# One DMA transpose per batch of the attention output, in place of one for each half of the heads

## The chip, the cores and the metric

One core of a Trainium2 chip runs the whole program. The metric is the device time of one execution in microseconds (us). The kernel before takes 726.11 us, the median of three runs (722.44, 726.11 and 727.01 us). The profiled execution took 723.2 us, and its span, from the first to the last instruction that the profile shows, is 721.4 us.

## The reference

Attention over 8 batches, 8 heads, 576 positions and 64 channels, with two kinds of mask, and after it a mixture of 8 experts in which each token goes to one expert and each expert takes 576 tokens:

```
mask_local = (rel >= 0) & (rel < 32)                        # heads 0 to 3
mask_strided = (rel >= 0) & (pos_k % 32 == pos_q % 32)      # heads 4 to 7
attn_out = softmax(mask(q k^T / 8)) v
x = attn_out.transpose(0, 2, 1, 3).reshape(4608, 512)       # one row per token
logits = x @ w_gate                                         # 4608 by 8
# pairs (token, expert) in falling order of logit; a pair is taken if the token
# is free and the expert has fewer than 576 tokens
out[mask_e] = relu(x[mask_e] @ w1[e]) @ w2[e]
```

Columns 0 to 255 of x come from the local heads and columns 256 to 511 from the strided heads.

## The kernel before, in words

**Units and steps.** The attention is cut into 16 units (`Unit`, L265): unit 2b is the four strided heads of batch b and unit 2b+1 its four local heads. Each unit is worked in two steps, one for each pair of heads. The loop at L609 runs over the steps i from -1 to 31, and everything in it is a schedule written out by hand: in step i TensorE does the scores of pair i+1 (`dots`, L353), the products with v of pair i (`mix`, L397), and the start of the scores of pair i+2. VectorE takes maxima (L357, L366), builds the shift (L371) and norms the result (L412 to L415); ScalarE takes the exponentials (L380). Work that belongs to no step of its own is put into lists by step (`at`, `drips`, `mids`, L530 to L565).

**What each unit moves.** `load` (L305) brings k, q and v for a unit three units ahead, at the start of an even step, on SP's queue (L312, L313, L319, L323). k and q of a kind have two buffers, and so has v, so a load must wait until the unit two of its kind before has been used. `finish` (L421) cuts the unit's result into a 16-bit high part and a low part (ScalarE L427, GpSimd L428). `store` (L430) writes both into the scratch tensor `x_scr` in HBM, whose row for a token holds 2 by 512 values: the second index of its shape is the column half, 0 for local and 1 for strided, and each half has 256 high and 256 low values. A strided unit's store is six transfers (L440), three from SP and three from GpSimd (four and two for the last strided unit); a local unit's is two from SP (L444, L445).

**The transposes.** `turn` (L447) reads a unit's half of the batch's rows back from `x_scr` as 576 by 512 and writes it transposed into an SBUF tile `xts` or `xtl` of 128 partitions by 4 by 576. One runs for each unit but the last: eight strided and seven local. `gates` (L459) multiplies both tiles of a batch with the gate's weights on TensorE (L465) and `logits` (L509) sums them up. The last batch's local half is transposed on TensorE (L481) instead, and its logits are made by `last_part` (L492).

**The order on SP's queue.** SP takes its instructions strictly in program order and stops at the first that has to wait. From the lists, the order for batches 0 to 4 is, over and over: transpose of strided unit 2b; store of local unit 2b+1; load of strided unit 2b+4; transpose of local unit 2b+1; store of strided unit 2b+2; load of local unit 2b+5. The lists put a unit's transpose four steps after the unit's first step for units 0 to 9, three for units 10 to 13 and one for unit 14 (L565). A batch's `gates` runs in step 4b+9 up to batch 4, in step 28 for batch 5 and in step 30 for batch 6.

**After the attention** comes a search for the expert's tokens (L768), then the experts one after another: the tokens are gathered (L1072), transposed 128 rows by 1024 at a time (L1075 by DMA, L1060 on TensorE), and multiplied (L1159, L1207), with the weights loaded and cut at L987 to L1021. The change doesn't touch this part.

Of the kernel before, what the change touches and what calls it, by code (L numbers as in the profile page):

```python
# [9 lines left out]
F16 = mybir.dt.float16  # L10
# [8 lines left out]
B, H, S, D = 8, 8, 576, 64  # L19
# [113 lines left out]
def band_stride_attention_then_capacity_moe(ctx, tc, qt, kl, ks, nl, ns, wg, w1, w2, cst, out, dbg=None):  # L133
    nc = tc.nc
# [8 lines left out]
    x_scr = dram.tile([N, 2, DM], F16, name="x_scr")  # L143
# [76 lines left out]
    with tc.tile_pool(name="ld", bufs=2) as ld, \  # L220
# [44 lines left out]
        class Unit:  # L265
# [71 lines left out]
            def room(u, p):  # L337
                u.sp[p] = ps_a.tile([128, 2, BANK], F32, name="spa")
# [106 lines left out]
                    nc.sync.dma_start(xs[n:, 0], xo[:S - n, n // 128])  # L445

            def turn(u):  # L447
                j = 1 if u.strided else 0
                u.xt = wk.tile([128, 2, 2, S], F16, name="xt" + u.g)
                nc.sync.dma_start_transpose(u.xt.rearrange("p a d n -> p (a d) n"), x_scr[u.b * S:(u.b + 1) * S, j])  # L450

        HB = S // 2
        ltb, gs = {}, {}
# [1 line left out]
        def gate_scale(b):  # L455
            gs[b] = wk.tile([128, 1], F32, name="st")
            nc.vector.tensor_scalar(gs[b], vscale[b][0][:, 1:2], sg[:, 1:2], None, op0=OP.mult)

        def gates(b, po):  # L459
            lt = ltb[b] = wk.tile([128, S], F32, name="lt")  # L460
            xts = (todo[2 * b + 1].xt, todo[2 * b].xt)
            for a in range(2):
                for j in range(2):
                    for k in range(4):
                        nc.tensor.matmul(po[32 * k:32 * k + 32, j, :HB], wgh[:, k].rearrange("p a e -> p (a e)"),  # L465
                                         xts[k // 2][:, a, k % 2, j * HB:(j + 1) * HB],
                                         start=(a == 0), stop=(a == 1), skip_group_check=True)
            nc.scalar.activation(lt.rearrange("e (j n) -> e j n", j=2), po[:, :, :HB], AF.Copy, scale=gs[b])
# [40 lines left out]
        def logits(b, po):  # L509
            po = po[:, :5 * E].rearrange("q (c e) -> q c e", e=E)  # L510
            sp = spans(b)
            for k, (r, _, tok) in enumerate(sp):
                nc.tensor.matmul(po[r, k], ltb[b][:, tok], sum_g, start=(k == 0), stop=(k == 4), skip_group_check=True)
            c = sp[0][1]
            nc.vector.tensor_copy(L[:, c:c + 4], po[:, :4])
            r, c, _ = sp[4]
            nc.vector.tensor_copy(L[r, c], po[r, 4])
# [8 lines left out]
        todo = [Unit(b, strided) for b in range(B) for strided in (True, False)]  # L526
        nu = len(todo)
        fills = {}

        def at(step, f, early=False):  # L530
            q = fills.setdefault(max(step, 0), [])
            q.insert(0, f) if early else q.append(f)
# [6 lines left out]
        for j, u in enumerate(todo):  # L539
            if j == 1:  # L540
                for k in range(6):
                    drips.setdefault(k // 3, []).append(lambda u=u, k=k: u.copy_v(k))
                for p in range(2):
                    drips.setdefault(2, []).append(lambda p=p: todo[0].rescale(p))
            if j > 1:
                if not u.strided:
                    for k in range(6):
                        drips.setdefault(2 * j + COPY_AT[k], []).append(lambda u=u, k=k: u.copy_v(k))
                    for f in range(2):
                        at(2 * j - V_AT + f, lambda u=u, f=f: u.square_v(f), True)  # L550
                else:
                    at(2 * j - V_AT_S, u.square_v, j > 2)
                if not u.strided:
                    mids2[2 * j - 3] = u
                    drips.setdefault(2 * j - 2, []).append(u.scale_v)
            if not u.strided and u.b < B - 1:
                at(2 * j + (4 if u.b < B - 2 else 3), lambda k=u.b: gate_scale(k))
                if u.b < B - 2:
                    mids.setdefault(2 * j + (7 if u.b < B_LATE else G5), []).append(lambda a, b, k=u.b: gates(k, a))
                (mids if u.b == B - 2 else mids3).setdefault(2 * j + (L_AT if u.b < B_LATE else G5 + 1 if u.b < B - 2 else 5), []).append(lambda a, b, k=u.b: logits(k, b))  # L560
            for p in range(2):
                at(2 * j + p if j else 2, lambda u=u, p=p: u.finish(p, nc.gpsimd))
            at(2 * j + (2 if j < nu - 2 else 1), u.store)
            if u is not todo[-1]:
                at(2 * j + (4 if j < 2 * B_LATE else 3 if j < nu - 2 else 1), u.turn)  # L565
        todo[0].load(v=False)
        for u in todo[:2]:
# [12 lines left out]
        def pair(i):  # L580
            return (todo[i // 2], i % 2) if 0 <= i <= last else None
# [27 lines left out]
        for i in range(-1, 2 * nu):  # L609
            u, n, m = pair(i), pair(i + 1), pair(i + 2)  # L610
# [7 lines left out]
            if m or i in mids:  # L618
                a = room(m) if m else ps_a.tile([128, 2, 512], F32, name="spa")
# [446 lines left out]
    def tokens(ph, idx):  # L1066
        xt = xp.tile([128, 2 * 2 * 2, CAP], F16, name="xt")
        for t in range(NT):
            n = min(128, CAP - 128 * t)
            xg = xp.tile([128, 2 * DM], F16, name="xg", bufs=5)  # L1070
            with urgent(ph):
                nc.gpsimd.indirect_dma_start(out=xg[:n], out_offset=None, in_=x_rows,  # L1072
                                             in_offset=bass.IndirectOffsetOnAxis(ap=idx[:n, t:t + 1], axis=0))
                if ph or t >= TURNS:
                    nc.sync.dma_start_transpose(xt[:, :, t * 128:t * 128 + n], xg[:n])  # L1075
                else:
                    first.append(lambda t=t, n=n, xg=xg: turn(xt, xg, t, n))
        return xt.rearrange("p (a j d) n -> p a j d n", a=2, j=2)
# [252 lines left out]
```

## Time and profile before

| | |
|---|---|
| median of 3 runs | 726.11 us |
| the profiled execution | 723.2 us |
| its span | 721.4 us |
| TensorE (PE) busy over the span | 625.3 us, 87% |
| VectorE, ScalarE, GpSimd busy | 455.9, 320.8, 153.7 us |
| mean granted clock of TensorE | 0.893 |
| the attention, by the last transposes of `last_part` (L496) | up to 220 us |
| transposes by `turn` (L450) | 8 + 7 on SP's queue |

How to read it. PE is TensorE's matmuls, PEld its weight loads, DVE VectorE, ACT ScalarE, POOL GpSimd and SP SyncE; a name with a q behind it (SPq, POOLq) is that engine's queue of DMA issues. L397 is line 397 of the kernel. In a row of waits the columns are the time waited in all, the number of times and the longest one. In a row of the timeline they are the start, the duration, the engine, the line, the operation, what is written and read, and in brackets the idle time in front of it and what ended it. In a row of the table by windows they are the window and its length, then the busy time of each engine with its number of instructions, the granted clock, the mean busy share of the 16 DMA engines and GB/s. Rows of DMA queues give packets, megabytes and the share of 16 engines' time that the packets took; it can pass 100% where packets overlap.

### The profile page before, as it was taken

The numbers are of one execution on the slowest core, as the hardware profiler recorded it, in microseconds if no ns is written. First come the engines' busy times: TensorE is split into PE (matmuls) and PEld (weight loads), VectorE is DVE, ScalarE is ACT, GpSimd is POOL, SyncE is SP. The second block draws the span as 40 slices with busy tenths as digits, with TensorE's granted clock in tenths as the row PEclk, the third lists the DMA queues.
The fourth block names the chain that finished last, engine by engine and source line by source line (L and its number), as shares of the span: only waits on it lengthen the run. The fifth ranks groups of instructions, "written<-read, shape, count | busy, mean of one in ns | idle before, by whom it ended". The sixth has DMA issues, their size and how long they took to land.

```text
span 721.4 us, 19211 instructions
## 1 busy us (share of the span) xinstructions
PE 625.3 (87%) x8040; PEld 402.7 (56%) x8043; DVE 455.9 (63%) x1368; ACT 320.8 (44%) x497; POOL 153.7 (21%) x152
## 2 busy tenths in 40 slices
PE   6986978889993479999989998989989998699993
PEld 3664756566663346557537646646644744555741
DVE  4786666786876777867657767757666573662200
ACT  3634634653520156473454364274184265753210
POOL 2053323332330020140040040041041023202011
PEclk9667787985885589999999999999999999899998
DMA  9999999999651360680680491392196079551010
GB/s 248 263 256 221 248 262 260 232 247 214 113 134 50 122 200 1 218 213 2 223 194 15 146 254 33 105 265 63 35 295 103 1 271 262 182 96 52 1 38 29
DMA packets 111401, 111.21 MB, mean 154 GB/s; under 512 B 76332, under 2 KB 84102, under 8 KB 110803
## 3 DMA queue, kind: packets, MB, share of 16 engines
q1 hardware_dynamic: 103235, 88.44, 47.7%
q0 software_dynamic: 7360, 21.15, 9.9%
q8 instruction: 63, 1.03, 0.6%
q10 hardware_dynamic: 720, 0.39, 0.2%
q14 instruction: 23, 0.19, 0.1%
HBM read 73.59 MB, written 18.87 MB: 128 GB/s over the span
## 4 chain that ended last, share of the span: by engine, by line
PE 29%; issue 16%; DVE 7%; DMA 6%; ACT 3%; SPq 3%; POOL 2%; another core or an unknown queue 1%; POOLq 0%; ACTq 0%
PE ph L1159 16%; PE ph L1207 9%; DMA w<-in_w_dram 4%; SPq L1075 2%; DVE w2l L1021 2%; ACT jk L1002 2%; DMA xg<-x_scr,idx 2%; POOL out_dram L1218 1%; DVE w1l L1021 1%; DVE hl L1167 1%; PE ph L1201 1%; POOL xg L1072 1%; SPq L987 1%; PE ph L1060 0%
## 5 line engine op out<-in xcount | busy, mean ns | idle before, releaser
L1159 PE MATMUL ph<-xt,w1h 128*128 128x288 f16 (+2 forms) x1024 | 180.0, 288 | 7.0 <-DMA xt<-xg 4.4
L1218 POOL DMA_INDIRECT out_dram<-y,idx x40 | 43.5, 1087 | 351.3 <-ACT y L1217 324.8
L1159 PEld LDWEIGHTS <-w1h 128*128 128x128 f16 x1024 | 97.1, 98 | 34.5 <-issue 6.7
L1159 PE MATMUL ph<-xt,w1l 128*128 128x288 f16 (+2 forms) x512 | 113.3, 288 | 0.0
L1002 ACT ACTIVATE jk<-w 128x1024 f16<-128x1024 f32 x64 | 67.5, 1055 | 73.2 <-DMA w<-in_w_dram 69.3
L1207 PE MATMUL ph<-w2l,hh 128*128 128x512 f16 x256 | 97.9, 382 | 0.0
L1207 PE MATMUL ph<-w2h,hh 128*128 128x512 f16 x256 | 97.7, 382 | 0.0
L1207 PE MATMUL ph<-w2h,hl 128*128 128x512 f16 x256 | 97.7, 382 | 0.0
L1166 ACT ACTIVATE hh<-ph 128x576 f16<-128x576 f32 (+2 forms) x72 | 42.8, 595 | 120.2 <-PE ph L1159 119.2
L1207 PEld LDWEIGHTS <-hh 128*128 128x128 f16 x512 | 48.7, 98 | 58.0 <-issue 9.5
L1167 DVE SCALAR_TENSOR_TENSOR hl<-ph,hh 128x576 f16<-128x576 f32 (+2 forms) x72 | 49.5, 688 | 43.7 <-ACT hh L1166 43.4
L380 ACT ACTIVATE pr<-spa 128x576 f32<-128x576 f32 x32 | 20.8, 650 | 93.9 <-PE spa L376 89.4
L1159 PEld LDWEIGHTS <-w1l 128*128 128x128 f16 x512 | 49.9, 98 | 12.6 <-issue 0.6
L397 PE MATMUL po<-v_s,pr 64*54 64x65 f32 (+1 forms) x768 | 45.6, 276 | 10.2 <-issue 6.5
L428 POOL TENSOR_TENSOR xos<-xs,xos 118x768 f16<-118x768 f32 x16 | 27.2, 1701 | 119.8 <-ACT xos L427 87.8
L1217 ACT ACTIVATE y<-ph,so 128x512 f32<-128x512 f32 x32 | 21.9, 684 | 67.7 <-PE ph L1207 48.1
L1072 POOL DMA_INDIRECT xg<-x_scr,idx x40 | 40.5, 1012 | 50.2 <-issue 34.7
L1021 DVE SCALAR_TENSOR_TENSOR w1l<-w,w_sw,w1h 128x512 f16<-128x512 f32 x64 | 45.7, 745 | 8.0 <-issue 4.6
L1021 DVE SCALAR_TENSOR_TENSOR w2l<-w,w_sw,w2h 128x512 f16<-128x512 f32 x64 | 45.7, 742 | 7.9 <-ACT y L1217 6.8
L397 PEld LDWEIGHTS po<-v_s,pr 64*54 64x54 f32 (+1 forms) x768 | 34.7, 162 | 17.2 <-issue 11.7
L1207 PEld LDWEIGHTS <-hl 128*128 128x128 f16 x256 | 25.1, 98 | 33.2 <-issue 8.1
L1020 ACT ACTIVATE w1h<-w,w_sw 128x512 f16<-128x512 f32 x64 | 41.8, 710 | 3.9 <-DVE ss_e L203 1.8
(613 smaller groups left out, 961.9 us busy)
## 6 DMA issues: line engine op xcount, KB each, us to landing
w<-in_w_dram SPq DMA_DIRECT2D x64, 512.0 KB
kl<-in_kl_dram SPq DMA_DIRECT2D x16, 304.0 KB
v_s<-in_ns_dram SPq DMA_DIRECT2D x16, 292.5 KB
v_l<-in_nl_dram SPq DMA_DIRECT2D x16, 292.5 KB
ks<-in_ks_dram SPq DMA_DIRECT2D x16, 288.0 KB
qs<-in_qt_dram SPq DMA_DIRECT2D x16, 288.0 KB
ql<-in_qt_dram SPq DMA_DIRECT2D x16, 288.0 KB
x_scr<-xol SPq DMA_DIRECT2D x8, 512.0 KB
```

The lines of the kernel that those rows point to most:

```text
L397: nc.tensor.matmul(po[r:r + n, j - j0], pr[k, o:o + n], u.vn[k, t, 2 * p + h], start=(j == j0), stop=(j == j1 - 1), skip_group_check=True)
L428: eng.tensor_tensor(u.xo[:nr, :, 1, c], xf, u.xo[:nr, :, 0, c], op=OP.subtract)
L1002: nc.scalar.activation(jk, wf[:, c * n4:(c + 1) * n4].rearrange("p c f -> p (c f)"), AF.Square, scale=1.41422, accum_out=sq[:, c:c + 1])
L1020: nc.scalar.activation(hi[:, c, f], wf[:, c, f], AF.Copy, scale=s_)
L1021: nc.vector.scalar_tensor_tensor(lo[:, c, f], wf[:, c, f], s_, hi[:, c, f], op0=OP.mult, op1=OP.subtract)
L1072: nc.gpsimd.indirect_dma_start(out=xg[:n], out_offset=None, in_=x_rows, in_offset=bass.IndirectOffsetOnAxis(ap=idx[:n, t:t + 1], axis=0))
L1159: nc.tensor.matmul(tile_[:, j, :w], wt[:, d, f * 128:(f + 1) * 128], xt[:, d // 2, xx, d % 2, c], start=(k == 0), stop=(k == 3 * DC - 1))
L1166: nc.scalar.activation(hv, src, AF.Relu)
L1167: nc.vector.scalar_tensor_tensor(lv, src, 0.0, hv, op0=OP.max, op1=OP.subtract)
L1207: nc.tensor.matmul(py, a[:, f, ts_], w[:, f], start=(k == 0), stop=(k == len(todo) - 1))
L1217: nc.scalar.activation(y, py, AF.Copy, scale=so[:, t:t + 1])
L1218: st = nc.gpsimd.indirect_dma_start(out=out_rows, out_offset=bass.IndirectOffsetOnAxis(ap=idx[:n, t:t + 1], axis=0), in_=y[:n], in_offset= ...
```

## The change

The transpose of a strided unit is dropped. When the local unit of the batch is due, one transpose reads both halves, 576 rows by 1024 values, and writes both into one tile `xt` of 128 partitions by 2 by 4 by 576, of which there are two buffers; `gates` reads its two halves as before. The two tiles of 4,608 bytes for each partition and two buffers each become one tile of 9,216 bytes with two buffers, so the room in SBUF is the same. The last strided unit, whose local half is never transposed by DMA, keeps its own transpose of 576 by 512.

```diff
             def turn(u):
-                j = 1 if u.strided else 0
-                u.xt = wk.tile([128, 2, 2, S], F16, name="xt" + u.g)
-                nc.sync.dma_start_transpose(u.xt.rearrange("p a d n -> p (a d) n"), x_scr[u.b * S:(u.b + 1) * S, j])
+                j = slice(1, 2) if u.strided else slice(0, 2)
+                xt = wk.tile([128, 2, 2, 2, S], F16, name="xt", bufs=2)
+                nc.sync.dma_start_transpose(xt[:, j].rearrange("p j a d n -> p (j a d) n"),
+                                            x_scr[u.b * S:(u.b + 1) * S, j].rearrange("n j f -> n (j f)"))
+                u.xt = xt[:, 1]
+                if not u.strided:
+                    todo[2 * u.b].xt, u.xt = xt[:, 1], xt[:, 0]
...
-            if u is not todo[-1]:
+            if not u.strided and u.b < B - 1 or j == nu - 2:
                 at(2 * j + (4 if j < 2 * B_LATE else 3 if j < nu - 2 else 1), u.turn)
```

On SP's queue the order becomes: store of local unit 2b+1; load of strided unit 2b+4; transpose of batch b; store of strided unit 2b+2; load of local unit 2b+5. Fifteen transposes become seven of double width and one of the old width.

## The prediction

> **What bounds the kernel now.** I read the page first, then the table by windows, the waits of TensorE, the timelines of TensorE and SP, and at last the DMA queues in short windows.
>
> ```profile
> PE 625.3 (87%) x8040; PEld 402.7 (56%) x8043; DVE 455.9 (63%) x1368; ACT 320.8 (44%) x497; POOL 153.7 (21%) x152
> DMA  9999999999651360680680491392196079551010
> q8 instruction: 63, 1.03, 0.6%
> ```
>
> The DMA engines are full in the first ten of 40 slices, up to 180 us. Queue 8 carries 63 packets, 1.03 MB: one packet of 16 KB for every 255 of TensorE's 16,083 instructions. I read it as TensorE's instruction fetch. Now a stretch around the transpose of local unit 1:
>
> ```profile
> 60.00:66.00 6.00, 5.49 (x175) 3.95 (x165) 5.65 (x17) 4.06 (x5) 3.79 (x4) 1.00 1.16 228
> 66.00:72.00 6.00, 0.23 (x7) 0.17 (x6) 1.82 (x7) 0.00 (x0) 0.72 (x1) 0.78 1.14 226
> 72.00:78.00 6.00, 6.00 (x121) 4.28 (x122) 3.02 (x6) 2.85 (x4) 0.15 (x1) 0.50 1.07 240
> ```
>
> TensorE sets the pace of the attention: where it runs it is busy for 5.5 to 6.0 of 6 us, longer than any of the others but VectorE in the first row. From 66 to 72 us it stands still, the others run out of work behind it, and afterwards its granted clock is half. The waits of TensorE between 40 and 170 us:
>
> ```profile
> PE po L397 <- issue: 10.2, 8, 5.8
> ```
>
> It waits for nothing that the profile names, in the middle of a group of like matmuls:
>
> ```profile
> 65.51 0.54 PE L397 MATMUL po<-v_s,pr 64*54 64x65 f32 x11
> 71.83 1.03 PE L397 MATMUL po<-v_s,pr 64*54 64x65 f32 x13 [5.77 <-issue]
> ...
> 94.23 0.25 PE L353 MATMUL spa<-qs,ks 64*18 64x18 f32 x4 [2.91 <-issue]
> ...
> 117.90 0.44 PE L353 MATMUL spa<-qs,ks 64*54 64x54 f32 x8 [1.56 <-DMA x_scr<-xos]
> ```
>
> The queues in four short windows, 61 to 69, 69 to 70.5, 86.2 to 91.5 and 91.5 to 93 us, in this order:
>
> ```profile
> q0 software_dynamic: 167, 0.28, 21.6%
> ...
> q8 instruction: 1, 0.02, 4.7%
> ...
> q1 hardware_dynamic: 2473, 1.45, 117.3%
> ...
> q0 software_dynamic: 182, 0.28, 53.1%
> ...
> q8 instruction: 1, 0.02, 4.2%
> ```
>
> In these windows a local transpose moves, by its 2,304 packets of 256 B from 62.5 to 69.5 and from 88.3 to 91.9 us. The first and the third window have no row of queue 8, so no fetch is served there; one comes as each transpose ends, takes 1.1 us (4.7% of 16 engines in 1.5 us), and TensorE goes on 2.3 us behind the end of the transpose (69.5 to 71.83, 91.9 to 94.23). In the third window GpSimd's stores, issued at 87.28 us, have no row either, and 182 packets right after it. So a transpose holds the DMA engines to its end, and TensorE runs out of instructions behind it. I take the wait before 117.90 us, behind the local transpose of batch 2, for the same, though the profile puts it down to a store. No stall of this list stands behind a strided transpose: there the fetch is late too, but TensorE still had instructions left.
>
> The Trainium skill (Runtime: NRT & Kernel Launch, Instruction fetch mechanics) says that instructions come in blocks of 16 KiB, 256 to a block, and that crossing into the next is mostly hidden. The trace agrees on the block; on the hiding it differs, by 5.77 us. If the page held here, the length of a transpose would cost nothing and the sum below would be 0.
>
> **The change part by part.** SP's queue around batches 0 and 1, then GpSimd's stores:
>
> ```profile
> 48.60 3.42 SPq L450 DMA_TRANSPOSE xts<-x_scr  x1
> 53.35 2.20 SPq L323 DMA_DIRECT2D v_s<-in_ns_dram  x4
> 58.77 5.51 SPq L450 DMA_TRANSPOSE xtl<-x_scr  x1
> ...
> 80.25 1.91 SPq L323 DMA_DIRECT2D v_s<-in_ns_dram  x4
> 84.44 5.90 SPq L450 DMA_TRANSPOSE xtl<-x_scr  x1
> ...
> 59.26 2.08 POOL L440 DMA_DIRECT2D x_scr<-xos  x3 [0.30 <-POOL xos L428]
> 87.28 1.99 POOL L440 DMA_DIRECT2D x_scr<-xos  x3 [0.30 <-POOL xos L428]
> ```
>
> *Data.* 576 by 512 values are 589,824 B, 2,304 packets of 256 B. 8 x 2,304 + 7 x 2,304 packets before, 7 x 4,608 + 2,304 after: the same 34,560, since a row is cut into 256 B either way. Its cost is not the bytes but how long one piece lasts.
>
> *Length of one piece.* An undisturbed one, 203.5 to 206.4 us, and the flow in 110.5 to 115.3 us:
>
> ```profile
> 203.50:206.40 2.90, 2.48 (x81) 2.15 (x84) 2.72 (x11) 1.34 (x2) 0.00 (x0) 0.91 1.00 203
> ...
> GB/s 384 365 346 384 422 365 442 384 384 365 442 384 365 442 365 365 326 405 341 303 233 230 190 164 68 30 36 28 203 292 288 292 288 292 288 292 288 292 288 292
> ```
>
> The flow dips, some 1.5 us, while engines finish their loads one by one, then runs at 290 GB/s. Another 589,824 B take 2.0 us at 290 GB/s. A double transpose lasts 4.9 us alone (2.9 + 2.0) and 5.6 under load (3.6 + 2.0). SP's issue grows from 2.29 us (the shortest) to between 2.29 and 4.58; I take 4.2, since a part is fixed.
>
> *What moves.* The strided transpose no longer stands ahead of the local store and the strided load. It waits for TensorE's last product of the unit two of its kind before, here units 2 and 4:
>
> ```profile
> 49.36 1.67 PE L397 MATMUL po<-v_s,pr 64*54 64x65 f32 x24
> ...
> 78.95 1.27 PE L397 MATMUL po<-v_s,pr 64*54 64x65 f32 x24
> ```
>
> Unit 4's ends at 80.2 us and the load goes out at 80.25: it is held by TensorE, not by SP. So in batches 1 to 4 it comes no earlier, though its data meet an emptier queue, which I put at 0.5 us. Unit 2's ends at 51.0 us and the load went out at 53.35: in batch 0 it can go 2.3 us earlier, and with the 0.5 us the transpose can start to move at 59.8 us in place of 62.5.
>
> *Stalls, batch by batch*, each from both sides:
>
> - Batch 0: now 5.8 us. This transpose took 7.0 us against 3.6 because GpSimd's stores (issued at 59.26) were under way and got between: 167 packets of queue 0 above. Started at 59.8 us it is ahead of them, as batch 1's was, starting 1.0 us behind the issue. Then it ends at 59.8 + 5.6 = 65.4 us, and TensorE, dry at 66.05, goes on at 67.7: 1.6 us, a gain of 4.2. If the stores get between after all: 2.0 us longer. Ends: -4.2 and +2.0; I take -4.2.
> - Batches 1 and 2: the end moves by 2.0 - 0.5 and the stall with it, one for one: +1.5 each, between 0 and +5 (2.0, and 3.4 for stores in between).
> - Batches 3 and 4: no stall stands behind their transposes now, so part of the 2.0 us is covered by what TensorE has left. Ends 0 and +2.0 each; I take +0.5 and +1.0.
> - Batches 5 and 6: the DMA engines are at half load there. 0 to +1 together; +0.5, half way.
>
> Sum: -4.2 + 1.5 + 1.5 + 0.5 + 1.0 + 0.5 = +0.8 us.
>
> *At nothing.* The strided half is later, but only `gates` reads it:
>
> ```profile
> 202.18 2.63 SPq L450 DMA_TRANSPOSE xtl<-x_scr  x1
> ...
> 209.43 0.42 PE L465 MATMUL spa<-xtl,wgh 128*32 128x288 f16 x2
> ```
>
> The schedule leaves three steps between a batch's transpose and its `gates` up to batch 4, and one for batch 6, the tightest: issued at 202.18, moving from 203.5, landed by 208.4 (203.5 + 4.9), used at 209.43; without that cover it costs up to 1 us, inside batch 6's bound. The store of unit 2b+2 and the local load behind the transpose go out up to 4.6 us later; but loads run three units ahead and the transpose of the strided unit that used to stand in front of the next ones is gone, so they are covered; if they were not, the delay would be those 4.6 us. SP's waits for strided stores ahead of a transpose vanish; nothing behind them was late.
>
> The profiled execution took 723.2 us, so the sum gives 724.0 us for it. That execution lies 2.9 below the median of 726.1, so I forecast 726.9 us for the median.
>
> **The rivals.**
>
> *Longer stalls (slower).* Batch 0 gains nothing because GpSimd's stores still get in, and each loaded double transpose puts its full 2.0 us on TensorE: 5 x 2.0 = 10.0 us. Two more stalls (batches 3 and 4) each bring a stretch at half clock: 121 matmuls in 6 us against 175, a loss of 1.9 us, together 3.7. Sum +13.7, about 740 us. For it: the stalls end with the transpose wherever it is seen. Against it: batches 3 and 4 had room left. It decides from the point where the stall in batch 0 is not below 5.8 us. In a mild form (+8) it gives 734.
>
> *Fetches slip in between (faster).* If the double transpose is served in pieces, the extra half adds no blocking: batches 1 to 6 add 0, batch 0 gains 4.2, and the half clock behind it (if 10 us at a loss of 1.9 in 6) goes too, 3.2. Sum -7.4, 718.7 us. For it: the flow dips at the start of each transpose, where others get in. Against: no queue-0 or queue-8 packet in the last 3 us of the one at 88.3 us.
>
> The Trainium skill (DMA: Bandwidth & Descriptors, Queues, rings and completion order) says that an engine goes round its queues packet by packet, at most 64 descriptors each, and so speaks for this rival. By it a fetch would wait for 64 descriptors at most, not for a whole transpose; no run here shows such a change of queue within the steady flow.
>
> *Nothing that can be told (no effect).* TensorE's stalls move about and come out even, or the one instruction is worked as two halves: 723 to 730 us. This holds my own sum too.
>
> **How the numbers follow.** The three runs differ by 4.6 us, so about 1%, 7.3 us, is what can be told from no change. My sum and its neighbours: 0.60. Longer stalls: 0.25, from the two batches in which the end of the transpose and of the stall are seen together. Fetches slip in: 0.15. Faster by over 1% is the second rival's 0.15, slower the first's 0.25. The range must reach into both: from 717 (the faster rival and 1.6 us of scatter) to 739 (the slower one, all but its last us).
>
> **What would show it.** Right: seven transposes of some 5 to 6 us of movement in the short windows, no queue-8 packet inside them and one right behind; the idle time in L397 near 66 us at 1 to 2 us in place of 5.77; those near 94 and 118 us longer by about 1.5 us; 34,560 packets as before; the last product of `gates` no later by more than 1 us against its neighbours. Wrong: stalls of 4 us or more behind most double transposes (the first rival), or queue-8 packets within them and stalls below 3 us (the second). If the stalls are as said and the time is still off by over 1%, the clock's half-rate stretches, which I have not put in the sum, are the first place to look.

## The result and the profile after

The changed kernel takes 734.17 us, the median of 4 runs (731.51 to 738.09). On the same chip the kernel before took 724.28 (720.55 to 727.01, 4 runs). The ratio is 1.0117 [1.0078, 1.0157]: 1.2% slower, more than the 1% that the prediction set as what can be told. The profiled execution took 734.62 us. Here and below a median is over all executions of a kernel, while a ratio leaves out those that lie more than 1.5% above the fastest of the same kernel.

First the page of the changed kernel, the lines that answer to those of before:

```profile
span 732.9 us, 19206 instructions
...
PE 629.6 (86%) x8040; PEld 405.2 (55%) x8043; DVE 458.1 (63%) x1368; ACT 320.4 (44%) x497; POOL 155.6 (21%) x152
...
DMA  9999979999653072291392293085078079551010
...
q8 instruction: 63, 1.03, 0.6%
```

The work is the same and as long as before; only the span is 11.5 us longer. The table by windows tells in which part. Its columns are: window, length, then busy time and count for PE, PEld, DVE, ACT and POOL, and last the granted clock, the DMA share and GB/s. I cut at the last product of `last_part`, where the attention ends. Before:

```profile
0.00:219.90 219.90, 184.47 (x4491) 133.20 (x4493) 158.37 (x425) 100.06 (x128) 69.20 (x70) 0.77 0.95 223
219.90:721.40 501.50, 440.81 (x3553) 269.50 (x3551) 297.49 (x944) 220.69 (x369) 84.48 (x82) 0.95 0.43 124
```

After:

```profile
0.00:232.10 232.10, 185.29 (x4490) 134.23 (x4492) 160.12 (x425) 99.71 (x128) 69.49 (x70) 0.79 0.88 211
232.10:732.90 500.80, 444.30 (x3554) 271.02 (x3552) 298.02 (x944) 220.69 (x369) 86.15 (x83) 0.94 0.43 124
```

All of it is lost in the attention, which ends 12.2 us later. TensorE is busy there for 0.8 us more; it stands idle for 46.8 us (232.10 - 185.29) in place of 35.4. So the loss is waiting. The waits of TensorE between 40 and 170 us, after the change (waited for, us in all, times, longest):

```profile
PE spa L353 <- issue: 12.5, 6, 5.2
PE po L397 <- issue: 6.7, 5, 2.9
PE spa L376 <- DVE dd L371: 6.7, 4, 3.3
```

The 10.2 us in L397, 5.8 of them in one piece, have shrunk, and more has come up at L353. Where, the timeline of TensorE shows (start, length, instruction, and in brackets the idle time before it):

```profile
64.78 1.08 PE L397 MATMUL po<-v_l,pr 64*32 64x65 f32 x29 [1.64 <-issue]
...
96.88 0.25 PE L353 MATMUL spa<-qs,ks 64*18 64x18 f32 x4 [5.22 <-issue]
...
121.53 0.32 PE L353 MATMUL spa<-qs,ks 64*54 64x54 f32 x8 [3.51 <-issue]
...
135.28 0.29 PE L397 MATMUL po<-v_s,pr 64*18 64x65 f32 x3 [2.87 <-issue]
...
178.48 0.82 PE L353 MATMUL spa<-qs,ks 64*54 64x54 f32 x22 [2.82 <-issue]
...
196.69 0.21 PE L397 MATMUL po<-v_l,pr 64*32 64x65 f32 x1 [1.80 <-issue]
```

Against the list of before: 1.64 for 5.77 (-4.1); 5.22 for 2.91, 3.51 for 1.56, 2.87 for 0.72 and 2.82 for 0.75 at the very same instructions (+2.3, +1.95, +2.15 and +2.07); one of 1.80 at an instruction that had none; and one of before that is gone:

```profile
139.84 0.30 PE L397 MATMUL po<-v_l,pr 64*32 64x65 f32 x3 [2.29 <-issue]
```

Together +3.9 of the 11.4 us of idle time that came on top. The rest is in several stalls of 1.0 to 1.5 us and in longer waits for VectorE's `dd` (8.1 us between 40 and 222 us, 5.0 before). Some of it is scatter: the first thing that differs on SP's queue is the strided transpose that was issued at 48.60 us, and yet the products of L376 that started at 45.54 us before start at 47.41 after. But the loss isn't from there. The group of 24 products (L397) that started at 78.95 us before starts at 77.87 after, so the changed kernel is still ahead then, and all of the loss comes between 78 us and the end of the attention.

Now batch 1, in which the transpose moves from 86.5 to 96.5 us by its packets of 256 B. The DMA queues of the changed kernel from 86.5 to 92 us (packets, MB, share of 16 engines), with the flow in 40 slices:

```profile
GB/s 376 361 281 332 264 188 155 73 56 17 34 17 34 9 17 30 270 296 287 285 294 294 289 285 294 294 289 283 296 313 302 270 89 39 76 290 291 283 289 263
...
q1 hardware_dynamic: 3944, 1.16, 127.4%
q0 software_dynamic: 8, 0.01, 0.6%
```

And from 92 to 96.6 us:

```profile
GB/s 341 289 292 343 187 25 31 45 38 22 7 9 414 89 127 236 94 52 185 298 384 289 402 340 183 214 263 134 107 80 112 131 53 27 18 38 0 145 196 317
...
q1 hardware_dynamic: 990, 0.45, 82.4%
q0 software_dynamic: 184, 0.28, 33.3%
q8 instruction: 1, 0.02, 1.5%
```

While the transpose flows at about 290 GB/s, GpSimd's queue 0 gets 8 packets in and the fetch none, though GpSimd issued its stores at 85.92. But the transpose is not done when they do get in. Of its 4,608 packets 4,302 have moved by 92.5 us; the last 306 take another 4.0 us. From 92 us on 184 packets of queue 0 are served. The fetch comes among them, at 94.4 us, and TensorE stands until 96.88. Batch 4 has the same picture, from 176 to 178 us:

```profile
q1 hardware_dynamic: 291, 0.16, 86.2%
q0 software_dynamic: 88, 0.13, 20.4%
q8 instruction: 1, 0.02, 3.2%
```

The transposes of batches 0 to 4 take 7.8, 10.0, 9.1, 7.3 and 9.3 us from first to last packet, where the prediction had 5.6. SP's queue shows it as well, in the issue of the transposes of batches 0 to 2:

```profile
56.96 8.83 SPq L450 DMA_TRANSPOSE xt<-x_scr  x1
...
82.68 8.68 SPq L450 DMA_TRANSPOSE xt<-x_scr  x1
...
113.21 8.46 SPq L450 DMA_TRANSPOSE xt<-x_scr  x1
...
123.33 1.13 SPq L319 DMA_DIRECT2D v_l<-in_nl_dram  x2
```

### The profile page after: what moved, and what is told of

Its sections match the earlier page's. It is cut to its first block, busy times and chain, and to the rows that moved or that the text cites. A ratio compares the mean times of both kernels' runs of the same rounds, so it can differ in the third digit from the quotient of the medians.

```text
span 732.9 us, 19206 instructions
## 1 busy us (share of the span) xinstructions
PE 629.6 (86%) x8040; PEld 405.2 (55%) x8043; DVE 458.1 (63%) x1368; ACT 320.4 (44%) x497; POOL 155.6 (21%) x152
## 3 DMA queue, kind: packets, MB, share of 16 engines
q1 hardware_dynamic: 103011, 88.44, 46.8%
## 4 chain that ended last, share of the span: by engine, by line
PE 24%; issue 18%; DMA 11%; DVE 6%; SPq 3%; POOL 3%; ACT 2%; POOLq 0%; DVEq 0%; ACTq 0%
PE ph L1163 18%; DMA w<-in_w_dram 5%; DMA xg<-x_scr,idx 3%; SPq L1079 3%; PE ph L1211 3%; DMA xt<-xg 2%; DVE w2l L1025 2%; POOL out_dram L1222 1%; POOL xg L1076 1%; ACT jk L1006 1%; SPq L991 1%; DVE hl L1171 1%; DVE w1l L1025 0%; PE ph L1064 0%; DVE y L1219 0%
## 5 line engine op out<-in xcount | busy, mean ns | idle before, releaser
L1163 PE MATMUL ph<-xt,w1h 128*128 128x288 f16 (+2 forms) x1024 | 183.9, 293 | 11.7 <-DMA xt<-xg 9.2
L1163 PE MATMUL ph<-xt,w1l 128*128 128x288 f16 (+2 forms) x512 | 114.9, 292 | 0.0
L397 PE MATMUL po<-v_s,pr 64*54 64x65 f32 (+1 forms) x768 | 41.6, 260 | 8.4 <-issue 3.9
L1024 ACT ACTIVATE w2h<-w,w_sw 128x512 f16<-128x512 f32 x64 | 41.1, 710 | 3.6 <-DVE w_sw L208 3.5
```

The source lines that it names most:

```text
L397: nc.tensor.matmul(po[r:r + n, j - j0], pr[k, o:o + n], u.vn[k, t, 2 * p + h], start=(j == j0), stop=(j == j1 - 1), skip_group_check=True)
L1024: nc.scalar.activation(hi[:, c, f], wf[:, c, f], AF.Copy, scale=s_)
L1163: nc.tensor.matmul(tile_[:, j, :w], wt[:, d, f * 128:(f + 1) * 128], xt[:, d // 2, xx, d % 2, c], start=(k == 0), stop=(k == 3 * DC - 1))
```

## The experiments

**The theory.** In its steady flow a transpose lets no other queue have a turn. A wide one lasts long enough that the stores that GpSimd issues near its start get in before it is done. They stretch it, and TensorE's fetch, and the loads behind it, come later still.

**The rivals.** It is width itself: twice the bytes in one piece keep the fetch out for longer, whatever the others do. Or it is the later place alone: the strided half now moves behind the local store, next to the local half. Each kernel below was timed in 5 rounds beside the kernel before; the ratios are to that. Diffs are against the changed kernel, unless it says otherwise.

**1. Two narrow transposes at the late place.** The place of the change, without its width.

```
-nc.sync.dma_start_transpose(xt[:, j].rearrange(...), x_scr[...rows of the batch, j].rearrange(...))
+for k in range(j.start, j.stop)[::-1]:
+    nc.sync.dma_start_transpose(xt[:, k].rearrange("p a d n -> p (a d) n"), x_scr[u.b * S:(u.b + 1) * S, k])
```

> The changed kernel with its wide transpose cut into two of 576 by 512, one behind the other at the same place, strided half first. Theory (a transpose holds the DMA engines from its start to its end, and TensorE's instruction fetch with them): what counts is how long the transposes move without a break. If the two run on without a break, 732 to 736 us as the changed kernel, with the stall near 94 us at 4 us or more; if a fetch gets in between them, 724 to 729 us. Rival (the place on SP's queue, 8.5 us of issue ahead of the local load): 732 to 736 us whether or not a fetch gets in between.

Measured: 722.32 us, 1.0019 [0.9984, 1.0054]. Its attention by windows:

```profile
0.00:220.80 220.80, 178.31 (x4491) 130.15 (x4493) 159.89 (x426) 99.67 (x128) 69.98 (x70) 0.81 0.95 222
```

The whole loss is gone with the same bytes at the same place, so the place is not the cause. What the border between the two halves does, the queues show at batch 0, from 64 to 65.5 us, when 2,304 packets have moved:

```profile
q1 hardware_dynamic: 1063, 0.27, 79.3%
q0 software_dynamic: 153, 0.24, 41.9%
```

And in batch 3, from 139.5 to 141.5, inside a pair that moves from 136.3 to 144:

```profile
q1 hardware_dynamic: 1280, 0.32, 78.6%
q0 software_dynamic: 192, 0.30, 39.3%
q8 instruction: 1, 0.02, 3.2%
```

The border is a door: stores and a fetch go through in the middle. It doesn't help each time: the pair of batch 1 moves for 9.8 us, its first half alone for 5.9. The fetch does go through behind that half, at 91.5 us, but TensorE has waited for 5.14 us when it goes on, as long as in the changed kernel. Of the 11.3 us by which the attention is shorter than the changed kernel's, 4.3 are idle time and 7.0 busy time of TensorE, at a granted clock of 0.81 in place of 0.79.

**2. Only the local half.** The strided half of batches 0 to 6 is left out, as the expectation says.

```
-j = slice(1, 2) if u.strided else slice(0, 2)
+j = slice(1, 2) if u.strided else slice(0, 1)
...
-todo[2 * u.b].xt, u.xt = xt[:, 1], xt[:, 0]
+todo[2 * u.b].xt, u.xt = xt[:, 0], xt[:, 0]
```

> The strided half is not transposed at all for batches 0 to 6: the one transpose at the late place is 576 by 512 of the local half, and the products with the gate's weights read that half twice. Theory: the strided transposes of the kernel before stalled nothing, so taking them away from it gains little: 720 to 726 us, and the step from here to the changed kernel, 8 to 14 us, is the price of the second half at this place. Rival (it is the place or the longer wait of the gate's products, not the length): 731 us or more.

Measured: 716.26 us, 0.9892 [0.9857, 0.9926]; attention's end at 217.9 us. Transposes of 3.1 to 4.4 us. That is below both ranges of the expectation. It shows how much hangs on the second half of the bytes, some 16 us between this kernel and the changed one, but not by which way.

**3. The changed kernel with all strided stores on SP.** This takes the stores away from GpSimd and keeps the width.

```
-q = nc.gpsimd if SR * f + k in (LATE_Q if u is todo[-2] else STORE_Q) else nc.sync
+q = nc.sync
```

> The changed kernel with all six transfers of a strided unit's store issued by SP, none by GpSimd. Theory of length alone: 731 to 736 us, since the wide transposes are as long. Rival (GpSimd's stores get in between the packets of a wide transpose and draw out its last part, seen from 92 to 96.5 us): the transposes last 5 to 6 us in place of 7 to 10, the stalls behind batches 1, 2 and 4 are 2 us shorter each, 725 to 729 us.

Measured: 721.22 us, 1.0000 [0.9962, 1.0038]. The transposes now move for 5.7, 7.9, 5.6, 5.7, 6.2, 6.3 and 6.0 us: the 5.6 of the prediction, but for batch 1. The attention by windows:

```profile
0.00:220.00 220.00, 177.78 (x4491) 128.71 (x4493) 160.45 (x428) 99.50 (x128) 53.69 (x47) 0.81 0.90 223
```

The longest stalls in TensorE's timeline:

```profile
68.08 1.03 PE L397 MATMUL po<-v_s,pr 64*54 64x65 f32 x13 [2.60 <-issue]
...
94.14 0.25 PE L353 MATMUL spa<-qs,ks 64*18 64x18 f32 x4 [3.15 <-issue]
...
113.30 0.70 PE L517 MATMUL spb<-sum_g,lt 128*128 128x8 f32 x4 [3.99 <-issue]
```

And the queues of its batch 1, from 84.9 to 92.7 us:

```profile
q1 hardware_dynamic: 4961, 1.60, 124.1%
q8 instruction: 1, 0.02, 0.8%
```

The stall behind batch 1's transpose is back to 3.15 us (5.22 in the changed kernel, 2.91 before). The width alone costs nothing that can be measured (the interval is 0.4% to either side); the rival that blames it falls. One thing to be careful with: against the changed kernel only 4.6 of the 12.1 us in which the attention is shorter are idle time (42.2 in place of 46.8); the other 7.5 are busy time of TensorE, at a granted clock of 0.81 in place of 0.79. Whether the clock follows from the fewer waits isn't shown by these runs.

**4. Later by two steps.** The wide transposes of batches 0 to 4, and what reads them, two steps of the schedule later, away from GpSimd's stores.

```
-B_LATE, L_AT, G5, GW_AT = 5, 8, 6, 4
+B_LATE, L_AT, G5, GW_AT = 5, 10, 6, 4
...
-mids.setdefault(2 * j + (7 if u.b < B_LATE else G5), [])...
+mids.setdefault(2 * j + (9 if u.b < B_LATE else G5), [])...
...
-at(2 * j + (4 if j < 2 * B_LATE else 3 if j < nu - 2 else 1), u.turn)
+at(2 * j + (6 if j < 2 * B_LATE else 3 if j < nu - 2 else 1), u.turn)
```

> The changed kernel with the wide transposes of batches 0 to 4 two steps later, where the next batch's strided transpose used to stand (behind the local load, ahead of the local store and the strided load), and the gate's products and logits of these batches two steps later too. Theory of length: the same length blocks as long, so 730 to 736 us. Rival (the place: only behind a strided load does TensorE's fetch come at a bad time, since no stall stood behind a strided transpose before): 722 to 728 us.

Measured: 721.64 us, 0.9942 [0.9898, 0.9986]; transposes of 5.9 to 7.2 us, with GpSimd's stores as they were. Once it starts when they are through, the wide transpose costs nothing. By the ratio this version is a little faster than the kernel before; by the medians the two are level (722.13 for the kernel before).

**5. The kernel before with all stores on SP.** The control for 3: the same line of the diff of 3, made in the kernel before.

```
-q = nc.gpsimd if SR * f + k in (LATE_Q if u is todo[-2] else STORE_Q) else nc.sync
+q = nc.sync
```

> The kernel before with all six transfers of a strided unit's store issued by SP. Theory (the loss of the changed kernel is GpSimd's stores getting in between the packets of its longer transposes): in the kernel before the stores meet a transpose in batch 0 alone (7.0 us against 3.6), so there is little to win here, 0.990 to 1.000. Rival (GpSimd's stores cost any kernel the same, and the wide transposes cost on top of that): 0.982 to 0.989, as far below the kernel before as the changed kernel with SP's stores lay below the changed kernel.

Measured: 728.17 us, 1.0019 [0.998, 1.0059]. Taking the stores from GpSimd gains nothing by itself. So in 3 it is worth 1.2% only because the transpose is wide: the two things have to meet.

**6. Both: later, and stores on SP.** The diffs of 3 and 4 together:

```
+q = nc.sync
...
+at(2 * j + (6 if j < 2 * B_LATE else 3 if j < nu - 2 else 1), u.turn)
```

> The wide transposes of batches 0 to 4 two steps later, the gate's products and logits too, and all stores by SP. If the later place was better only because GpSimd's stores don't fall into its transposes: the same as the wide one with SP's stores at the first place, 0.996 to 1.002. If the place itself is better for TensorE's fetches: as the later place with GpSimd's stores or below, 0.985 to 0.995.

Measured: 720.41 us, 0.9939 [0.9894, 0.9983], the same as 4. Where the place keeps the stores away, taking them from GpSimd adds nothing. But the ratio lies in the range that was given for the place itself being better (0.985 to 0.995), not in that for the stores alone (0.996 to 1.002). So the later place may have a gain of its own of about 0.6%; that the two cures are wholly for the same thing isn't shown.

**7. The pair at the late place, stores on SP.** The diffs of 1 and 3 together; beside 3 it tells the price of the width where nothing disturbs it:

```
+q = nc.sync
...
+for k in range(j.start, j.stop)[::-1]:
+    nc.sync.dma_start_transpose(xt[:, k].rearrange("p a d n -> p (a d) n"), x_scr[u.b * S:(u.b + 1) * S, k])
```

> Two transposes of 576 by 512 one behind the other at the late place, all stores by SP. Theory of GpSimd's stores: without them nothing is left between one wide and two narrow transposes, so the same as the wide one with SP's stores, 0.996 to 1.004. Rival (an undisturbed wide transpose still keeps TensorE's fetch out 2 us longer than two narrow ones, which let it in between): 2 to 6 us faster than the wide one with SP's stores, 0.990 to 0.996.

Measured: 724.45 us, 0.9992 [0.9949, 1.0035], against 1.0000 in 3: no price that these intervals could tell.

**8. The changed kernel again**, without an edit, in as many rounds as the others.

```
 (no line changed)
```

> The changed kernel as it is, beside the three below, so that all are compared on one chip. If the first measurement holds, a ratio to the kernel before of 1.008 to 1.016; if it was the scatter of four runs, 0.997 to 1.006.

Measured: 738.65 us, 1.0129 [1.0084, 1.0174]; attention's end at 233.4, transposes of 7.6, 10.2, 8.5, 8.5 and 9.2 us. The loss and the stretch are there again.

**9. The wide transpose cut by rows into two** of 288 by 1024, so that a border lies in the middle, at another place than in 1, and GpSimd keeps its stores.

```
+w = S // 2
+for k in range(0, S, w):
+    nc.sync.dma_start_transpose(xt[:, j, :, :, k:k + w].rearrange(...), x_scr[u.b * S + k:u.b * S + k + w, j].rearrange(...))
```

> The changed kernel with each wide transpose cut by rows into two of 288 by 1024, one behind the other, GpSimd's stores as they are. Theory (TensorE's fetch is kept out while one transpose instruction moves, GpSimd's stores draw a wide one out, and a border between two instructions is a door for the fetch): a door in the middle as with two of 576 by 512, 0.998 to 1.005. Rival (it is the width of 1024 values, or the whole time that the transposes move, doors or not): 1.009 to 1.017 as the changed kernel.

Measured: 721.17 us, 0.9961 [0.9919, 1.0003]. The attention by windows, and the waits of TensorE between 40 and 222 us:

```profile
0.00:219.50 219.50, 181.39 (x4492) 130.52 (x4492) 160.96 (x425) 99.61 (x128) 69.42 (x70) 0.80 0.95 223
```

```profile
PE po L397 <- issue: 7.5, 6, 2.7
PE spa L353 <- issue: 5.0, 4, 1.7
```

And the queues from 91 to 92 us, at the border in the transpose of batch 1:

```profile
q0 software_dynamic: 147, 0.23, 73.4%
q1 hardware_dynamic: 156, 0.04, 30.5%
q8 instruction: 1, 0.02, 6.7%
```

Stores and the fetch go through at the border; 2,309 more packets of under 512 B, about half of a transpose, move behind it, from 92 to 96 us. The stall here is 1.34 us, and the longest of all 2.7. The two parts together still move for 7.4 to 8.4 us, in the mean of batches 0 to 4 for 8.1, and the pairs of 1 for 8.3; in the changed kernel it is 8.7. So the time from first to last packet is not what tells these kernels apart. What does is a door in the middle, by which the fetch needn't wait for the end.

**10. Cut into four** of 144 by 1024.

```
-w = S // 2
+w = S // 4
```

> The same, cut into four of 144 by 1024. Theory: three doors in place of one, 0.992 to 1.002, fetches at most some 3 us late. Rival (each new transpose pays the dip at its start, some 1.5 us, in which engines wait for each other): 4.5 us a batch longer on the DMA engines, the local loads later, 1.004 or more.

Measured: 722.35 us, 0.9971 [0.993, 1.0012]; attention's end at 224.0. More doors than one bring nothing further.

**11. Four parts at the later place**, the diffs of 4 and 10 together:

```
+w = S // 4
...
+at(2 * j + (6 if j < 2 * B_LATE else 3 if j < nu - 2 else 1), u.turn)
```

> Both at once: the transposes of batches 0 to 4 two steps later, and each wide transpose cut into four of 144 by 1024; GpSimd's stores as they are. If the gain of the later place and that of the doors are separate: 0.986 to 0.993. If both are the same gain (fetches in time): 0.991 to 0.997 as the later place alone.

Measured: 724.07 us, 0.9895 [0.984, 0.995]. The two numbers don't agree: by the ratio this version is 1% faster than the kernel before, by the medians it is level (723.21 for the kernel before). So the loss is gone here as well, but a gain over the kernel before isn't shown, and what the two parts add to each other isn't told.

**12. All six strided stores on GpSimd**, which doubles what the theory blames.

```
-q = nc.gpsimd if SR * f + k in (LATE_Q if u is todo[-2] else STORE_Q) else nc.sync
+q = nc.gpsimd if SR * f + k in range(2 * SR) else nc.sync
```

> The changed kernel with all six transfers of a strided unit's store issued by GpSimd: the suspected cost doubled. Theory (their packets get into the wide transposes and draw them out): the transposes of batches 0 to 4 move for 9 to 14 us, the attention ends later than the changed kernel's, 1.016 to 1.035. Rival (the changed kernel loses by something else on SP's queue, such as the three stores ahead of the local load): 1.005 to 1.014, since SP has three transfers less to issue.

Measured: 732.16 us (6 runs), 1.0109 [1.005, 1.0168]. By its time this is a miss for the theory: no more loss than in the changed kernel, and a ratio in the range of the rival. The rival's ground, the stores on SP ahead of the local load, doesn't bear it out either: with all six on SP (3) there was no loss. The transposes of batches 0 to 4 moved for 10.9, 7.5, 9.5, 6.6 and 10.9 us, three of the five in the 9 to 14 that the theory gave. The attention did grow:

```profile
0.00:237.10 237.10, 188.86 (x4493) 136.02 (x4493) 162.39 (x428) 99.85 (x128) 84.85 (x95) 0.76 0.87 207
```

Its end is 5.0 us later than in the changed kernel, but its part after the attention was 488.9 us in this execution, 12 us shorter than the 500.8 there. One profile doesn't tell which of the two is chance, and that doubling the stores costs more stays unproved.

**Together.** One profile each; idle time of TensorE in the attention is the end less the busy time. Left out are 2, which reads half of the data, and 5 and 11, of which there is no profile that can be set beside these:

| kernel | ratio | attention's end, us | TensorE idle in it, us |
|---|---|---|---|
| before | 1 | 219.9 | 35.4 |
| changed | 1.0117 | 232.1 | 46.8 |
| changed again (8) | 1.0129 | 233.4 | 45.3 |
| all on GpSimd (12) | 1.0109 | 237.1 | 48.2 |
| pair, late (1) | 1.0019 | 220.8 | 42.5 |
| stores on SP (3) | 1.0000 | 220.0 | 42.2 |
| pair, stores on SP (7) | 0.9992 | 219.8 | 35.2 |
| two by rows (9) | 0.9961 | 219.5 | 38.1 |
| four by rows (10) | 0.9971 | 224.0 | 40.8 |
| later (4) | 0.9942 | 220.9 | 35.4 |
| later, stores on SP (6) | 0.9939 | 219.6 | 41.0 |

The three kernels that have an undivided wide transpose beside GpSimd's stores are the three slow ones, by time, by the end and by idle time. Whatever parts the two, a border by columns, a border by rows, the queue of the stores or a later place, takes the whole loss away.

The idle time carries only a part of this: against 1, 3 and 9 the changed kernel has 4.3, 4.6 and 8.7 us more of it, of 11.3, 12.1 and 12.6 us of attention. The rest is busy time of TensorE, which differs as much between profiles of kernels with one and the same time. So that the pairing of the two costs 1.2% is shown; that all of it passes through late fetches is not.

What stays open: whether the later place has a gain of its own (its attention ends no earlier in single profiles); why doubling GpSimd's stores doesn't raise the time; and batch 2, below.

## Why the prediction was right in its range and wrong in its likeliest case

The time of 734.17 lies in the range, and the case that came is the slower rival in its mild form, 734, to which the text gave 0.25. The likeliest case, no change, did not come: the 726.9 us of the forecast were missed by 7.3, and the range holds because it was drawn up to the slower rival. That 734 is met so closely is luck in part. The kernel before took 724.28 us here and not 726.11, so the change is +9.9 us, not +8.

- *Bytes and packets: right.* The trace has 68,352 packets of 256 B before and after, the expert layers' included. The bytes cost nothing.
- *The length of one piece: the step that failed.* "A double transpose lasts 4.9 us alone (2.9 + 2.0) and 5.6 under load (3.6 + 2.0)": it lasted 7.3 to 10.0 us in batches 0 to 4. Where no GpSimd store meets it, it lasted 5.6 to 6.3 in experiment 3, but for 7.9 in batch 1, and 5.9 to 7.2 in experiment 4. The reason behind the number was "So a transpose holds the DMA engines to its end". That holds for the steady flow only. In its last part the flow falls off, to some 25 GB/s in batch 1, and others get in: 184 packets of queue 0. The prediction had seen this in batch 0 of the kernel before and kept a bound of 3.4 us for it, but took the value without it.
- *Batch 0: right in size* (-4.1 for -4.2), with stores as forecast: no packet of queue 0 from 58 to 66 us, and 192 from 66 to 69, as the flow ends. But the transpose lasted 7.8 us, and the stall that is left lies one block of instructions earlier than the old one; a fetch got in at 62 us, ahead of the steady flow. That this batch gained is luck in part as well: in the second measurement of the same kernel (8) the stall stands at the old instruction again and lasts 3.42 us:

```profile
70.17 1.03 PE L397 MATMUL po<-v_s,pr 64*54 64x65 f32 x13 [3.42 <-issue]
```

- *Batches 1 and 2: too small* (+2.3 and +1.95 for +1.5 each), inside the bounds. Batch 1 is shown above. In batch 2 the transpose is stretched as well (9.1 us), but the fetch came at 119.0 us, in mid-flow after 1,503 packets, and TensorE went on 2.5 us later. The flow ran on to 119.5 us and then all but stood for 1.3; the fetch itself took 1.0. From 118 to 121 us:

```profile
GB/s 41 17 218 297 287 287 297 290 287 290 294 287 294 505 266 273 280 259 273 266 20 10 0 0 0 0 0 7 7 10 7 10 10 10 7 10 10 10 188 290
```

  So the stretched tail doesn't explain this stall, and that no fetch gets into the steady flow isn't true without exception. Why it was served just then is open.
- *Batch 4: too small* (+2.07 for +1.0). The fetch stands in the stretched tail.
- *Batch 3: wrong.* The kernel before had a stall there, the 2.29 us before 139.84, while the batch's local transpose moved (137.3 to 141.0). The prediction passed over it, and it is gone. What has grown is the stall before 135.28 us (+2.15), and it comes ahead of batch 3's transpose: the fetch at 132.9 us shares its time with the local load for unit 11, which landed from 125 to 132.5, since it was issued behind a transpose that held SP for 8.46 us (113.21; the load at 123.33). (The loads around the transpose of batch b are those of strided unit 2b+6 and local unit 2b+7, not of 2b+4 and 2b+5 as in the order on SP's queue above.) That this load is what kept the fetch waiting is read from the times alone. "Covered", the word of the prediction for loads up to 4.6 us later, was so for the data and not for what these loads run into.
- *Batches 5 and 6: too small* (+1.8 for +0.5), above the bound of +1.
- *SP's issue: wrong*, 8.5 us under load against a bound of 4.58. The rows that the prediction shows of narrow transposes, 5.51 and 5.90, lay above this bound already. SP is held for about as long as the transpose moves.
- *The strided load is held by TensorE: right.* The wait of SP for TensorE's last product, 4.2 us before, is now the longest of its list between 40 and 222 us, and the wait for strided stores ahead of a transpose, 13.6, is gone:

```profile
SPq L323 <- PE po L397: 31.3, 5, 9.5
```

- *`gates` in time: right.* No wait of TensorE for a transpose stands in its list. Its three slots after a transpose are enough.
- *The rival "longer stalls"* has the sum right, by another way. It let the stores get between in batch 0 and set its deciding point there, "not below 5.8 us"; batch 0 went well here, and the stores got in in batches 1 to 4 (192, 192, 158 and 192 packets of queue 0 between the first and the last packet of the transpose; 77 in batch 0).
- *The rival "fetches slip in between"* fell: batch 1 shows 3,944 packets with no fetch in 5.5 us, and behind the one that slipped in, in batch 2, TensorE had still waited for 3.51.
- *The Trainium skill's rule* (DMA: Bandwidth & Descriptors, Queues, rings and completion order), by which an engine goes round its queues after at most 64 descriptors: the steady flow of batch 1 differs, with 8 packets of queue 0 among 3,944 of queue 1. Batch 2's fetch in mid-flow is the one row that speaks for it. The Trainium skill's other rule, that instruction fetch is mostly hidden (Runtime: NRT & Kernel Launch, Instruction fetch mechanics), differs from stalls of up to 5.22 us here.
- *The half clock*, left out of the sum, was no part of the result: 0.77 before and 0.79 after in the attention, with TensorE's busy time within 0.8 us. It is part of experiment 3, as said there.

With GpSimd's stores out of the way the forecast of no change is what was measured, 1.0000. That is agreement in the time; the sum's single terms weren't met there either (the stall in batch 0 is 2.60 against 1.6, a new one of 3.99 stands at 113.30).

## What to carry to other kernels

Fewer and larger DMAs are not a gain in themselves: count how long one of them keeps the other queues out, the instruction fetch among them, and what is issued from another queue while it runs. If a long transpose meets stores from GpSimd, give it a border in the middle, move the stores to the queue of the transpose, or start it when they are through; each of the three took back 1.2% here. And when you cost a transfer by its shortest undisturbed rows, look for the row where it was disturbed and ask whether the longer one will not be disturbed each time.

## What the runs showed of the hardware

- A transpose in its steady flow moves about 290 GB/s and lets next to nothing else in: 8 packets of queue 0 and no fetch beside 3,944 of its queue in batch 1. In batch 2 one fetch got in, and the flow then all but stood for 1.3 us. A border between two transposes lets 153 packets of queue 0 through within 1.5 us.
- TensorE runs dry at fixed places: the twelve stalls of this kind that I counted lie at the same count of instructions (matmuls, weight loads and semaphore instructions), 192 past a multiple of 256. It goes on 2.3 to 2.8 us after the packet of its fetch starts (69.2 to 71.83 before, 119.0 to 121.53 after).
- The issue of a transpose on SP lasts about as long as the transpose moves (8.5 us for a wide one under load that moves for 9.1, 2.2 for the last narrow one that moves for 2.55), so whatever SP issues behind it waits with it.
- TensorE's busy time in the attention isn't a constant of the kernel: 177.8 us at a granted clock of 0.81, 188.9 at 0.76. Between single profiles this alone makes 7 to 11 us.
